# Retention and gated feed-forward on one core: eighteen sums of weight quarters dealt out anew on VectorE, and one ScalarE copy placed behind two one-column copies

## The chip, the core and the metric

The kernel runs on one core of a Trainium2 chip. A core has TensorE for matrix products (PE in the profile; its weight loads are listed apart as PEld), VectorE (DVE), ScalarE (ACT), GpSimd (POOL) and SyncE (SP, which here only issues transfers). Each engine takes its instructions in the order in which the program gives them and holds an instruction until what it needs is there. The metric is the device time of one launch in microseconds (us); lower is better.

## The reference

Two layers. The first is a retention layer: for each of 8 batches and 8 heads, 576 tokens of 64 columns, scores of queries and keys, weighted with a decay that is nought above the diagonal, times the values. The second is a feed-forward layer over the 4608 tokens that come of it, with a sigmoid gate.

```
scores = scale * np.matmul(q, k.transpose(0, 1, 3, 2))
gamma = 1.0 - 2.0 ** (-5.0 - np.arange(H, dtype=np.float32))
Dmat = np.where(rel >= 0, gamma[:, None, None] ** rel[None, :, :], 0.0)
attn_out = np.matmul(scores * Dmat[None, :, :, :], v)
x = np.ascontiguousarray(attn_out.transpose(0, 2, 1, 3)).reshape(B * S, H * D)
gate = 1.0 / (1.0 + np.exp(-(x @ w_gate)))      # 4608 x 512 times 512 x 1536
out = (gate * (x @ w_val)) @ w_out              # 4608 x 1536 times 1536 x 512
```

## The kernel before

**Retention.** The decay is split into a factor for each query and one for each key, which are multiplied into q and k when they are cast to bf16 (`cast_pair`, `cast_qk`). What is left of it is a mask of zeros and ones. Work goes by chunks of 128 tokens: products of k and q (`row`), the mask on VectorE (`mask`, L654; for the first three pairs of chunks `pair_qk`, L462), the product with v inside the chunk (`intra`, L665), a product with the running state of the chunks before (`inter`, L681), and a sum into that state (`add_state`, L774 to L780). The first three pairs of chunks are worked off before the loop; the third pair is prepared in lines 1448 to 1503. Its k, q and v are cast (`kp`, `qp`, `vp`), its masked scores are the tiles `ptp`, and `third_intra` (L533) is the product that reads them. `pair_st` (L476) is the product of `vp` and `kp`.

**Feed-forward.** The first 512 tokens are done by `h_both` and `op_first`. Behind them come blocks: two of 256 tokens (from token 512 and 768; numbers w = 0 and 1 in the loop of L1526) with plain products, then blocks of 512 tokens in which each product of two by two quarters is made of seven quarter products instead of eight. These want sums of quarters of the operands. The sums of weights are made once:

- `w_sums(kind, i, u, engine)` (L343, recorded as L349) makes the i-th sum of gate weights (kind g, tile `wgt_sb`) or of value weights (kind w, tile `wvt`) for the u-th third of the hidden columns. Each is one VectorE operation over 128x512 bf16.
- `wo_sums(i, u, 3)` (L316, recorded as L322) does the same for a third of the output weights (tile `wt_sb`).
- For i = 0, 1, 3 the sum goes to a tile of its own. The one with i = 2 is made in place on the weights and comes later, at the places listed in `PLACES`; the change leaves these.

**The order of VectorE's work.** `w_sums("g", i, 0)` and `("g", i, 1)` are made while the first 512 tokens are done (`step_sums`). Lines 1461 to 1463 make the three `("w", i, 0)`, ahead of the first output products and so ahead of the third pair's masks in VectorE's queue. The other eighteen stand in the list `weight_sums` (L1516). A block of 256 tokens runs through 18 turns (i = 0 to 17): twelve of hidden products (`h_units`, products `h_g` and `h_v`, VectorE's product L896) and six of output products (`op_units`, L1229). In each odd turn of w = 0 and w = 1 one sum is taken from the list (L1546). In the same turns the loop hands out the retention's pieces: a slot (`slot`) with its products and masks, and in the turns behind it the copies of the slot's values out of two PSUM banks (`leave_own` L750 on ScalarE, `leave_other` L766 on VectorE) and the state sums. The next slot's `intra` writes the same two banks.

**A block of 512 tokens.** `ORDER` (L1088) is a list written out by hand: products, sums, casts and cues. The entry `o` takes the next half of one of the output's seven products (`quarters`, L1127), in the order 1, 2, 6, 5, 7, 3, 4, into two banks a and e. `keep("16", a)` and `keep("5", e)` are ScalarE copies of 128x512 (L1139) from a bank to SBUF, which VectorE adds later (L1144). The entry `A` is a cue: the loop then gives two retention chunks (`slot_of_two`): `intra` and a part of `inter`, then two copies of a single column each on ScalarE (`glance`, L709), then the next chunks' scores, then the rest of `inter`. That rest writes the banks which the glances read, so TensorE does it only behind them. The second cue of a block comes right behind the second half of product 5.

The lines at the centre:

```
for i in (0, 1, 3):                                        # L1462
    w_sums("w", i, 0, nc.vector)
weight_sums = [... for kind, u in (("w", 1), ("g", 2), ("w", 2)) for i in (0, 1, 3)]
weight_sums += [lambda u=u, i=i: wo_sums(i, u, 3) for u in range(3) for i in (0, 1, 3)]
if w < 2 and i % 2 == 1 and weight_sums:                   # L1546
    weight_sums.pop(0)()
yield from product(5, e, True)                             # L1177
keep("5", e)
yield tail
```

Of the kernel before, what the change touches and what calls it, by code (L numbers as in the profile page):

```python
# [16 lines left out]
def kernel(  # L17
# [19 lines left out]
    nc = tc.nc  # L37
# [1056 lines left out]
    def quarters(gvs, sums, t0, k):  # L1094
# [38 lines left out]
        tail = W * (k * NFC // 2 - (k * NFC // 4 if k > 1 else 0))  # L1133
# [3 lines left out]
        def keep(name, ps):  # L1137
            kept[name] = sum_tile([P, 2, W], FP32, f"s{name}_{t0}", of=KEPT)[:, 0:k]
            nc.scalar.copy(out=kept[name], in_=ps)  # L1139
# [28 lines left out]
        if not final:  # L1168
            yield from product(2, e, False)
            for b in range(k):  # L1170
                obs[b] = osb.tile([P, DM], FP32, tag="osb", name=f"ob_{t0 + b * P}")
                nc.scalar.copy(out=obs[b][:, 0:W], in_=e[:, b])
            yield tail
            yield from product(6, a, False)
            keep("16", a)
            yield tail
            yield from product(5, e, True)  # L1177
            keep("5", e)
            yield tail
            yield from product(7, a, False)  # L1180
            add_half(1, 1, a, "5")
            yield tail
            yield from product(3, e, False)
            add_half(0, 1, e, "16")
            for b in range(k):
                stored(obs[b], places(b))
            yield tail
            yield from product(4, a, False)
            for b in range(k):
                nc.scalar.copy(out=obs[k + b][:, 0:W], in_=a[:, b])  # L1190
                stored(obs[k + b], places(k + b))
            ffn_psum.order = ffn_psum.held[::-1] + [x for x in ffn_psum.order if x not in ffn_psum.held]
            ffn_psum.held = []
            yield tail
            return
# [263 lines left out]
    step(units, 2)  # L1459
    loads_to(1)  # L1460
    value_sums_begin()
    for i in (0, 1, 3):  # L1462
        w_sums("w", i, 0, nc.vector)

    def op_first(fcs, nbs, opps):
        for fc in fcs:
# [46 lines left out]
    store(opps[3], 3 * P, on_act)  # L1513
    casts_to(1)

    weight_sums = [lambda kind=kind, u=u, i=i: w_sums(kind, i, u, nc.vector) for kind, u in (("w", 1), ("g", 2), ("w", 2)) for i in (0, 1, 3)]  # L1516
    weight_sums += [lambda u=u, i=i: wo_sums(i, u, 3) for u in range(3) for i in (0, 1, 3)]

    SPARE = {}
    for at, kind, u in PLACES:  # L1520
        SPARE.setdefault(at, []).append((lambda u=u: wo_sums(2, u, 3)) if kind == "o" else (lambda kind=kind, u=u: w_sums(kind, 2, u, nc.vector)))
# [4 lines left out]
    for w, (t0, n) in enumerate(BLOCKS):  # L1526
# [16 lines left out]
            twos = []  # L1543

        for i, cols in enumerate(ffn_units(t0, n, nxt)):
            if w < 2 and i % 2 == 1 and weight_sums:  # L1546
                weight_sums.pop(0)()
            if w == 1 and i == n_h + TURN_AT:
                turn_step(7)
            for x in SPARE.get((w, i - n_h if w == 1 else i), ()):  # L1550
                x()
            gone += cols
            pieces += 1
            if stores and (nxt is None or w + 2 == len(BLOCKS) and pieces % 4 == 0):
                leave()
            if n > 256 and i % 2 and i < n_h:
                continue
            if pending:
                pending.pop(0)()
            elif slots < end and gone * (end - begin) >= (slots - begin) * (total - 5 * 2048):  # L1560
                next_slot(slots)
                valued = slots - 1
                slots += 1
            elif twos and (cue if n == 512 else i - n_h >= 1):
                cue.clear()
                next_two(*twos[0], n == 512)
                valued = twos[0][0][-1]
                slots = max([slots] + [s + 1 for s in twos.pop(0)[1]])
# [34 lines left out]
```

## Time and profile before

| What | Value |
|---|---|
| median of 3 runs | 311.48 us (309.74 to 311.97) |
| the profiled execution, its own time | 310.14 us |
| span of the profiled execution | 308.4 us |
| TensorE busy | 297.8 us (97%) |
| VectorE busy | 248.7 us (81%) |
| ScalarE busy | 199.7 us (65%) |
| GpSimd busy | 208.2 us (67%) |
| first 512 tokens' output, third pair | about 38 to 52 us |
| blocks of 256 tokens (w = 0, w = 1) | about 52 to 72 us and 72 to 91 us |
| blocks of 512 tokens | from 91 us to the end |

Times inside the profile count from the span's start. A line of the timeline gives start, length, engine, line of the kernel, operation, what is written and read, the shape, the count of merged instructions, and in brackets the idle time of the engine before it with what ended it. A line of the waits gives the total, the number of times and the longest. Lengths of TensorE's pieces are modelled and overlap; the distance between two starts is the safer measure.

### The profile page before, as it was taken

The numbers are of one execution on the slowest core, as the hardware profiler recorded it, in microseconds if no ns is written. First come the engines' busy times: TensorE is split into PE (matmuls) and PEld (weight loads), VectorE is DVE, ScalarE is ACT, GpSimd is POOL, SyncE is SP. The second block draws the span as 40 slices with busy tenths as digits, with TensorE's granted clock in tenths as the row PEclk, the third lists the DMA queues.
The fourth block names the chain that finished last, engine by engine and source line by source line (L and its number), as shares of the span: only waits on it lengthen the run. The fifth ranks groups of instructions, "written<-read, shape, count | busy, mean of one in ns | idle before, by whom it ended". The sixth has DMA issues, their size and how long they took to land.

```text
span 308.4 us, 10693 instructions
## 1 busy us (share of the span) xinstructions
PE 297.8 (97%) x4361; PEld 243.0 (79%) x4370; DVE 248.7 (81%) x488; ACT 199.7 (65%) x454; POOL 208.2 (67%) x254
## 2 busy tenths in 40 slices
PE   8999999999999998999999999999999999999994
PEld 7664456867858887887888788888888888888883
DVE  5947966896899899689888988898789968945893
ACT  6755464536548665965796579757965796658640
POOL 5765655654566699669966996699769916751490
PEclk9999999999999999999999999999999999999999
DMA  7999999997999996994299729972871392012004
GB/s 212 315 364 374 359 287 241 221 189 169 216 213 233 257 203 120 284 238 109 55 253 223 157 47 275 199 170 38 207 184 23 38 294 84 2 53 88 1 3 136
DMA packets 144994, 55.00 MB, mean 178 GB/s; under 512 B 124336, under 2 KB 136880, under 8 KB 144944
## 3 DMA queue, kind: packets, MB, share of 16 engines
q1 hardware_dynamic: 144144, 53.66, 70.9%
q8 instruction: 34, 0.56, 0.7%
q10 hardware_dynamic: 800, 0.66, 0.7%
q14 instruction: 16, 0.13, 0.1%
HBM read 37.75 MB, written 9.44 MB: 153 GB/s over the span
## 4 chain that ended last, share of the span: by engine, by line
PE 81%; DVE 8%; SPq 4%; DMA 2%; issue 2%; POOL 1%; ACT 1%; DVEq 0%; ACTq 0%; POOLq 0%
PE wa L1015 11%; PE gatea L1015 11%; PE qa L1127 11%; PE qe L1127 8%; PE we L1015 6%; PE gatee L1015 5%; PE op L1468 3%; PE h_v L891 3%; PE h_g L891 3%; PE hv L1319 3%; PE wg L1015 3%; SPq L188 3%; PE gateg L1015 3%; PE hg L1319 2%; PE op L1229 2%; DMA wg<-in_moe_w_gate_dram 2%
## 5 line engine op out<-in xcount | busy, mean ns | idle before, releaser
L409 POOL TENSOR_TENSOR qk<-k,ktab 128x512 bf16<-128x512 f32 x30 | 32.4, 1080 | 22.0 <-DMA k<-in_k_dram 19.8
L1015 PEld LDWEIGHTS <-wg_sb 128*128 128x128 bf16 x336 | 32.7, 98 | 4.9 <-PE op L1229 0.8
L1127 PEld LDWEIGHTS <-gsum 128*128 128x128 bf16 x336 | 31.9, 98 | 5.6 <-issue 0.7
L1015 PEld LDWEIGHTS <-wv_sb 128*128 128x128 bf16 x336 | 32.8, 98 | 4.2 <-issue 0.3
L952 POOL TENSOR_TENSOR gsum<-gv 128x256 bf16<-128x256 bf16 (+1 forms) x34 | 25.9, 770 | 12.6 <-DVE gv L1038 11.4
L409 POOL TENSOR_TENSOR qk<-q,qtab 128x512 bf16<-128x512 f32 x28 | 31.2, 1115 | 1.7 <-DMA q<-in_q_dram 1.6
L1015 PEld LDWEIGHTS <-wgt_sb 128*128 128x128 bf16 x252 | 24.6, 98 | 4.0 <-issue 1.2
L654 DVE TENSOR_TENSOR pt<-row,tri 128x256 bf16<-128x256 f32 x60 | 21.4, 412 | 7.5 <-PE row L647 7.5
L1015 PEld LDWEIGHTS <-wvt 128*128 128x128 bf16 x252 | 24.6, 98 | 2.9
L952 POOL TENSOR_TENSOR gsum<-gv,gsum 128x256 bf16<-128x256 bf16 x39 | 26.9, 719 | 0.0
L1038 POOL TENSOR_TENSOR gv<-gv,wu 128x512 bf16<-128x512 bf16 x7 | 8.1, 1162 | 27.4 <-DVE wu L1064 27.4
L1127 PEld LDWEIGHTS <-gv 128*128 128x128 bf16 x240 | 22.9, 98 | 3.7 <-issue 0.8
L1015 PE MATMUL wa<-xsum,wv_sb 128*128 128x256 bf16 x168 | 25.2, 273 | 0.1
L1015 PE MATMUL gatea<-xsum,wg_sb 128*128 128x256 bf16 x168 | 24.1, 273 | 0.0
L615 ACT CAST sb<-s 128x256 bf16<-128x256 f32 x46 | 18.2, 414 | 5.7 <-DVE s L778 3.1
L729 ACT CAST xT<-val 128x256 bf16<-128x256 f32 x50 | 15.7, 387 | 6.4 <-PE val L681 6.4
L946 POOL TENSOR_TENSOR gsum<-gv 128x256 bf16<-128x256 bf16 (+1 forms) x16 | 14.4, 908 | 7.8 <-DVE gv L1038 7.8
L1038 POOL TENSOR_TENSOR gv<-gv,ws 128x512 bf16<-128x512 bf16 x14 | 16.3, 1164 | 2.6 <-DVE ws L1067 2.6
L1059 DVE TENSOR_TENSOR gatee<-gatea,gs 128x512 f32<-128x512 f32 x14 | 9.8, 697 | 9.6 <-PE gatea L1015 6.3
L1067 DVE TENSOR_TENSOR ws<-wa,ws 128x512 f32<-128x512 f32 x21 | 14.4, 685 | 3.9 <-PE wa L1015 3.9
L1067 DVE TENSOR_TENSOR gs<-gatea,gs 128x512 f32<-128x512 f32 x21 | 13.8, 687 | 4.4 <-PE gatea L1015 3.6
L1036 ACT ACTIVATE gv<-gs 128x512 bf16<-128x512 f32 x21 | 13.0, 629 | 6.5 <-DVE gs L1067 6.5
(182 smaller groups left out, 851.8 us busy)
## 6 DMA issues: line engine op xcount, KB each, us to landing
k<-in_k_dram SPq DMA_DIRECT2D x26, 256.0 KB, 4.0
q<-in_q_dram SPq DMA_DIRECT2D x26, 256.0 KB, 3.9
v<-in_v_dram SPq DMA_DIRECT2D x26, 256.0 KB, 4.2
out_dram<-ob SPq DMA_DIRECT2D x25, 256.0 KB, 3.1
wg<-in_moe_w_gate_dram SPq DMA_DIRECT2D x12, 256.0 KB, 5.2
wv<-in_moe_w_val_dram SPq DMA_DIRECT2D x12, 256.0 KB, 5.2
wo<-in_moe_w_out_dram SPq DMA_DIRECT2D x12, 256.0 KB, 5.0
v32p<-in_v_dram SPq DMA_DIRECT2D x6, 256.0 KB, 4.8
```

Source lines behind the costliest of these rows:

```text
L409: eng.tensor_tensor(out=natural_qk[s][:, i].rearrange("p m (y d) -> p y m d", y=2), in0=by_halves(loaded[s][1 - i]), in1=tab, op=ALU.mult)
L615: eng(out=state[key], in_=src)
L654: nc.vector.tensor_tensor(out=probs[s][:, y], in0=row_ps[s][y][:, 0], in1=tri.unsqueeze(1).to_broadcast([P, M, 64]), op=ALU.mult)
L729: nc.scalar.copy(out=x_out(ALL, cols_of(s, i)), in_=x_in(val_ps[s][i], cols_of(s, i)))
L891: nc.tensor.matmul(ps[:, i], lhsT=w_sb[:, kc, (fc + i) * P:(fc + i + 1) * P], rhs=xT(kc, slice(t0, t0 + n)), start=(kc == 0), stop=(kc == ...
L946: eng.tensor_tensor(out=s3, in0=a11, in1=a21, op=ALU.subtract)
L952: eng.tensor_tensor(out=to, in0=a, in1=b, op=op)
L1015: nc.tensor.matmul(ps[:, f], lhsT=w[:, kc, f * P:(f + 1) * P], rhs=x[:, kc], start=(first and f == 0 and kc == 0), stop=(f == 1 and kc == ...
L1038: eng.tensor_tensor(out=to, in0=to, in1=src, op=ALU.mult)
L1067: nc.vector.tensor_tensor(out=me["s5"], in0=a, in1=me["s5"], op=ALU.add)
L1127: nc.tensor.matmul(ps[:, b], lhsT=left(fp)[:, b * P:(b + 1) * P], rhs=right(fp), start=(first and fp == 0 and b == 0), stop=(fp == NFC // ...
L1319: nc.tensor.matmul(ps, lhsT=(wg_sb if what == "g" else wv_sb)[:, kc, fc * P:(fc + 1) * P], rhs=xT(kc, slice(0, 4 * P)), start=(kc == 0), s ...
```

## The change

1. The three `("w", i, 1)` are made together with `("w", i, 0)`, ahead of the first output products, and leave the list.
2. The list then holds fifteen sums: `("g", 2)`, `("w", 2)`, and nine of the output weights. They are taken at named turns instead of at each odd one: in w = 0 at 1, 3, 5, 9, 11, 13, 15, 16, 17, in w = 1 at 1, 3, 5, 7, 9, 11. So turn 7 of w = 0 loses its sum, turn 16 has one in addition, and the turns 13, 15 and 17 of w = 1 have none. At w = 0, turns 1, 3, 5 now make `("g", 2)` where `("w", 1)` was, and 9, 11, 13 make `("w", 2)`; the turns 15, 16, 17 make the first third of the output weights' sums.
3. In all blocks of 512 tokens but the last, `keep("5", e)` stands behind the yield that follows product 5. What the loop gives at that yield, the two glances among it, comes ahead of it in ScalarE's queue.

```diff
@@ quarters
             yield from product(5, e, True)
+            yield tail
             keep("5", e)
-            yield tail
             yield from product(7, a, False)
@@ before the first output products
     value_sums_begin()
-    for i in (0, 1, 3):
-        w_sums("w", i, 0, nc.vector)
+    for u in range(2):
+        for i in (0, 1, 3):
+            w_sums("w", i, u, nc.vector)
@@ ahead of the loop over the blocks
-    weight_sums = [lambda kind=kind, u=u, i=i: w_sums(kind, i, u, nc.vector) for kind, u in (("w", 1), ("g", 2), ("w", 2)) for i in (0, 1, 3)]
+    weight_sums = [lambda kind=kind, u=u, i=i: w_sums(kind, i, u, nc.vector) for kind, u in (("g", 2), ("w", 2)) for i in (0, 1, 3)]
     weight_sums += [lambda u=u, i=i: wo_sums(i, u, 3) for u in range(3) for i in (0, 1, 3)]
 
+    SUMS_AT = {0: (1, 3, 5, 9, 11, 13, 15, 16, 17), 1: (1, 3, 5, 7, 9, 11)}
@@ in the loop
         for i, cols in enumerate(ffn_units(t0, n, nxt)):
-            if w < 2 and i % 2 == 1 and weight_sums:
+            if i in SUMS_AT.get(w, ()) and weight_sums:
                 weight_sums.pop(0)()
```

## The prediction

> **What bounds the kernel now.** I read the page's first part first, then what TensorE waits for, then the timeline at each of those waits and at each place that the change touches.
>
> ```profile
> span 308.4 us, 10693 instructions
> ...
> PE 297.8 (97%) x4361; PEld 243.0 (79%) x4370; DVE 248.7 (81%) x488; ACT 199.7 (65%) x454; POOL 208.2 (67%) x254
> ```
>
> TensorE works without a break almost everywhere: 97% of the span. None of TensorE's work is removed, added or reordered here. So the change can give only what TensorE now loses in waiting at the touched places, and can cost only what new waiting it makes. The waits of TensorE, in the view of who waited for whom:
>
> ```profile
> PE val L681 <- ACT glance L709: 0.8, 1, 0.8
> PE qa L1127 <- DVE gsum L952: 0.8, 2, 0.6
> ...
> PE val L665 <- ACT xT L750: 0.4, 1, 0.4
> ...
> PE gatea L1015 <- DVE s L778: 0.4, 1, 0.4
> ...
> PE gatee L1015 <- DVE gatee L1059: 0.2, 1, 0.2
> ```
>
> All but the second (feed-forward sums, in the blocks of 512) lie in the stretch from 58 to 119 us, each at or behind something that is moved. These four add up to 1.8 us, 0.6% of the span: this is the size of the question. The losses behind a wait are a little larger than its idle time, as the first place shows.
>
> **Place one: the sum that leaves turn 7 of the first block of 256.** Timeline, an undisturbed slot first, then the disturbed one:
>
> ```profile
> 57.32 1.04 PE L891 MATMUL h_v<-xT,wv_sb 128*128 128x256 bf16 x8
> ...
> 58.29 0.32 PE L665 MATMUL val<-pt,v 64*64 64x64 bf16 x16
> ...
> 58.43 0.30 PE L681 MATMUL val<-T,sb 64*64 64x64 bf16 x16
> ...
> 61.57 1.04 PE L891 MATMUL h_v<-xT,wv_sb 128*128 128x256 bf16 x8
> 61.63 0.86 DVE L349 TENSOR_TENSOR wgt_sb<-wg_sb 128x512 bf16<-128x512 bf16 x1
> 61.77 0.60 ACT L894 ACTIVATE gv<-h_g 128x512 bf16<-128x512 f32 x1 [0.21 <-PE h_g L891]
> ...
> 62.73 0.27 ACT L750 CAST xT<-val 128x128 bf16<-128x128 f32 x1 [0.36 <-DVE xT L766]
> ...
> 63.04 0.54 PE L665 MATMUL val<-pt,v 64*64 64x64 bf16 x16 [0.44 <-ACT xT L750]
> ...
> 63.40 0.32 PE L681 MATMUL val<-T,sb 64*64 64x64 bf16 x16
> ```
>
> From the start of `h_v` to the start of `inter` it takes 1.11 us undisturbed (57.32 to 58.43) and 1.83 here (61.57 to 63.40): 0.72 lost. The rows name the cause: the sum of 0.86 us stands ahead of VectorE's copy out of the value banks, ScalarE's copy waits for that one, and the next chunk's product wants the banks. Without the sum, VectorE's copy starts at 61.63. ScalarE's still stands behind the sigmoid that ends at 62.37, so it ends near 62.6; the undisturbed `val` would start at 61.57 + 0.97 = 62.54. That leaves 0.07: the place gives **0.65** (bounds 0.3 and 0.72; the lower one if VectorE's copy is met by another delay of half the size of the sum's).
>
> **Place two: the value-weight sums in the turns 9, 11, 13.** The same dependence comes again one slot later, where a sum stays in front of the copies:
>
> ```profile
> 66.56 0.42 DVE L349 TENSOR_TENSOR wgt_sb<-wg_sb,wgt_sb 128x512 bf16<-128x512 bf16 x1
> ...
> 67.53 0.54 PE L665 MATMUL val<-pt,v 64*64 64x64 bf16 x16
> ...
> 67.88 0.25 PE L681 MATMUL val<-T,sb 64*64 64x64 bf16 x8
> ```
>
> From `val` to `inter` it takes 0.35 here against 0.14 at 58.29: the second bank is already late. Turn 11 now gets the second sum of `wvt` in place of this third one of `wgt_sb`; its form's shortest and longest are in the view by source line:
>
> ```profile
> L349 DVE TENSOR_TENSOR wvt<-wvt,wv_sb x3: 547/712/733, 39.8 to 69.6; 128x512 bf16<-128x512 bf16 x3
> ```
>
> So it is 0.13 to 0.31 us longer, and this falls on the path: I take a **cost of 0.2** (bounds 0 and 0.31). The extra sum of turn 16 lies in the output products of this block, ahead of an idle time of VectorE:
>
> ```profile
> 73.69 0.76 DVE L654 TENSOR_TENSOR pt<-row,tri 128x256 bf16<-128x256 f32 x2 [2.29 <-PE row L647]
> ```
>
> It lasts 0.4 to 1.26 us (below) and 2.29 us hide it. Cost 0; were that cover gone, its whole length would come onto the mask.
>
> **Place three: the end of the second block of 256.**
>
> ```profile
> 68.57 3.40 PE L1229 MATMUL op<-wo_sb,gv 128*128 128x512 bf16 x15 [0.16 <-issue]
> ...
> 71.81 1.04 PE L891 MATMUL h_g<-xT,wg_sb 128*128 128x256 bf16 x8
> ...
> 87.30 3.40 PE L1229 MATMUL op<-wo_sb,gv 128*128 128x512 bf16 x15 [0.16 <-issue]
> ...
> 88.86 1.26 DVE L322 TENSOR_TENSOR wt_sb<-wo_sb,wt_sb 128x512 bf16<-128x512 bf16 x1
> ...
> 90.49 0.42 DVE L778 TENSOR_TENSOR s<-s,row 128x256 f32<-128x256 f32 x1
> ...
> 91.06 1.03 PE L1015 MATMUL gatea<-xT,wg_sb 128*128 128x256 bf16 x8 [0.36 <-DVE s L778]
> ...
> 92.30 1.26 DVE L322 TENSOR_TENSOR wt_sb<-wo_sb,wt_sb 128x512 bf16<-128x512 bf16 x1
> ...
> 95.74 0.60 PE L1015 MATMUL gatee<-xT,wgt_sb 128*128 128x256 bf16 x4 [0.15 <-DVE gatee L1059]
> ```
>
> Fifteen output products take 3.24 from start to next start (68.57 to 71.81), so `gatea` was due at 87.30 + 3.24 = 90.54 and came at 91.06: 0.52 lost, to a state sum that ends at 90.91. The sum at 88.86 goes; the state sum then ends at 90.91 - 1.26 = 89.65 and is 0.9 early. At 95.74 `gatee` waits 0.15 more for an addition of VectorE, which by then is 2.5 us ahead, since the sum at 92.30 goes too. What is late next are the ScalarE copies that the same addition wants, and no row has TensorE waiting for them here. The place gives 0.52 + 0.15 = **0.67** (bounds 0.36, the idle time of the first wait alone, and 0.67).
>
> **Place four: the copy behind the looks.**
>
> ```profile
> 117.47 0.59 ACT L1139 COPY s<-qe 128x512 f32<-128x512 f32 x1
> ...
> 117.94 0.23 ACT L709 COPY glance<-val 128x1 f32<-128x1 f32 x2
> ...
> 118.23 0.32 PE L681 MATMUL val<-T,sb 64*64 64x64 bf16 x16 [0.78 <-ACT glance L709]
> ...
> 118.62 1.20 ACT L729 CAST xT<-val 128x256 bf16<-128x256 f32 x4 [0.45 <-PE val L681]
> ```
>
> The copy of bank `qe` stands in ScalarE's queue ahead of the glances. It is the one that moves, and the next ScalarE operation starts 0.47 later than it (117.47 to 117.94). So the glances start 0.47 earlier and TensorE goes on **0.47** earlier; the remainder of its 0.78 stays with what ScalarE has ahead of both. The added wait: the moved copy now stands behind glances that wait for TensorE's `inter`, and behind the copy stand ScalarE's four copies out of the value banks (118.62). They have 0.45 of idle ahead of them, which takes in nearly all of the 0.47. The moved copy's own readers, VectorE's additions and product 3 into bank e, come behind product 7. In the waits view this is the only glance that TensorE waits for, so the five other blocks give 0 (bounds 0 and 0.3 together, one or two of them at a wait of 0.2, the least that the rows above show).
>
> **Place five: three more sums ahead of the third pair's masks.**
>
> ```profile
> 39.31 0.42 DVE L349 TENSOR_TENSOR wvt<-wv_sb 128x512 bf16<-128x512 bf16 x1
> 39.37 0.83 POOL L312 CAST wo_sb<-wo 128x512 bf16<-128x512 f32 x1 [0.62 <-DMA wo<-in_moe_w_out_dram]
> ...
> 40.51 0.43 DVE L349 TENSOR_TENSOR wvt<-wv_sb,wvt 128x512 bf16<-128x512 bf16 x1
> ...
> 41.48 1.26 POOL L393 CAST vp<-v32p 128x512 bf16<-128x512 f32 x2
> ...
> 43.04 2.48 DVE L462 TENSOR_TENSOR ptp<-qkp,trip 128x512 bf16<-128x512 f32 x4 [2.11 <-PE qkp L455]
> ...
> 43.05 0.42 PE L476 MATMUL st<-vp,kp 64*64 64x64 bf16 x16
> ...
> 46.74 0.64 PE L533 MATMUL pvp<-ptp,vp 64*64 64x128 bf16 x32
> ```
>
> The three present ones take 39.31 to 40.94, 1.63 us. VectorE is idle for 2.11 us ahead of the masks, so three more end near 42.6 and the masks are not touched. At the longest form in the trace, 1.26 each, they would end at 44.7, the masks at 47.2, and `pvp` would be 0.5 late. The nearer cover is that of GpSimd: its two casts of `vp` end at 42.74, and `st` wants them at 43.05, 0.31 later. Beside the present sums a cast of the same shape takes 0.83, alone 0.63 (half of 1.26), so two of them may end 0.4 later, 0.1 past `st`. I take a **cost of 0.2**, since the cast that runs before them is lengthened too (bounds 0 and 0.5, the lock below apart; a gain is out, as nothing is taken away here).
>
> The Trainium skill, SBUF — State Buffer, section Who interferes with whom, says that a VectorE operation with both inputs in SBUF contends with a GpSimd operation that reads SBUF, and that the one that comes second is blocked outright. The 0.83 against 0.63 agrees in direction; by the rule the cost of this place would be nearer to the lock below than to 0.2.
>
> **The sum.** -0.65 + 0.2 - 0.67 - 0.47 + 0.2 = **-1.39 us**; with all bounds at their good ends -2.16 (0.72, 0.67, 0.47, 0.3 and no costs), with all at their bad ends -0.3 (0.3, 0.36 and 0.47, less 0.31 and 0.5). The profiled execution took 310.14 us, 1.74 more than its span; less 1.39 that is 308.75. It was 1.34 below the median of the runs shown, from which the same sum gives 310.1. I predict **309.4**, the middle of the two; the middle of the two times of before is 310.8.
>
> **The rivals.**
>
> *The gain is taken in again* (change 0, 310.8 by the same middle). TensorE comes earlier to the blocks of 512, and something there that does not move with it, a load or a GpSimd cast, makes it wait. For it: such a wait is there already, the 0.8 of `qa` for `gsum`. Against: it is the only one of that kind among the waits quoted, so at most it hides a part; and among those of TensorE from 40 us on no load is named.
>
> *The lock.* Sums and casts at place five run strictly one after the other. The three forms at their shortest are 0.42, 0.55 and 0.43, 1.4 together; `vp` then ends at 44.1 and `st` is 1.1 late in place of 0.2: 309.4 + 0.9 = 310.3. For it: the lengthened cast. Against: the cast that ran from 39.37 into the present sums was 0.2 longer, not longer by a whole sum.
>
> *The copy behind the looks becomes the bound* (slower). If in a block the moved copy delays ScalarE's copies by its full 0.59, and these delay TensorE through the value banks or the next block's first products, it costs 0.59 in each of six blocks, 3.5 in all: 309.4 + 3.5 = 312.9, or 2.1 us slower than before. It outweighs the gains of 1.39 from the third such block on. For it: the chain of dependence exists. Against: the 0.45 of idle ahead of those copies, which leaves 0.14 of the 0.59, 0.84 in six blocks.
>
> *More than the sum.* Every feed-forward sum that TensorE waits for (0.8 in the waits view) comes in time as well, and the five other looks give their 0.3: 1.1 more, 308.3. For it: VectorE comes freer out of the small blocks. Against: those two waits lie in blocks where the change moves nothing.
>
> **How the numbers follow.** Forecast 0.56, gain taken in 0.16, lock 0.10, copy 0.10, more 0.08. Within 1% (3.1 us) is about what a measurement of this kernel cannot tell from no change, and the runs shown already spread by 2.2. Faster by over 1% needs 3.1 us: the last rival's 2.5 and the forecast reach it only with the spread of the runs: 0.14. Slower by over 1% is the copy rival with more than 0.59 per block or an unforeseen wait: 0.09. Within 1%: 0.77. The range runs from 307.4, about the last rival from the lower profiled execution (310.14 - 2.5 = 307.6), to 311.7, which takes in the two rivals near no change with the runs' spread and leaves out the copy.
>
> **What would show it.** Right: at the slot near 62 us `val` follows `h_v` in about 0.97; at the end of the second small block `gatea` follows the outputs without a wait; the glances of the first block of 512 stand ahead of the `qe` copy and TensorE's wait there is near 0.3. The second `wvt` sum lies ahead of the late bank near 67 us, 0.2 worse. Wrong: a wait of `st` for `vp` of over 0.5, `pvp` waiting for masks, ScalarE's `xT` copies gating a product, or a stretch beyond 130 us that has become longer.

## The result, and the profile after

The changed kernel takes 309.01 us (median; 306.98 to 312.77), the kernel before, run beside it, 311.05 (309.17 to 312.32). The ratio is 0.9924 [0.9897, 0.9952]: 2.0 us less by the medians, 2.4 by the ratio, which leaves out two slow executions of the changed kernel (312.00 and 312.77). The forecast was 309.4 and 1.39 less. The profiled execution of the changed kernel took 309.74 us, span 308.0; that of before 310.14, span 308.4. So this pair of profiles differs by 0.4 us only, and one term in it has the opposite sign to the forecast.

The page's first part of the changed kernel, and then what its TensorE waited for (total, times, longest):

```profile
span 308.0 us, 10701 instructions
...
PE 297.9 (97%) x4370; PEld 243.1 (79%) x4370; DVE 251.9 (82%) x488; ACT 199.1 (65%) x454; POOL 206.7 (67%) x254
```

```profile
PE val L665 <- ACT xT L750: 1.2, 2, 1.0
...
PE qa L1127 <- DVE s L780: 0.9, 1, 0.9
PE qe L1127 <- issue: 0.9, 1, 0.9
...
PE val L681 <- ACT glance L709: 0.2, 1, 0.2
```

Of the four waits that the forecast rested on, both of the gate products are gone and the one behind the looks is down from 0.8 to 0.2. But `val` waits 1.0 at the place where the wait should have gone, and two waits near 144 and 176 us are longer. The pair of profiles stage by stage, each number the distance between two starts on TensorE, worked out from the timelines:

| From, to | before | after | difference |
|---|---|---|---|
| first output product to the first block of 256 (place five) | 13.67 | 13.66 | -0.01 |
| first block of 256 (places one, two) | 19.78 | 20.56 | +0.78 |
| second block of 256 up to `gatea` (place three) | 19.25 | 18.77 | -0.48 |
| `gatea` (91.06 before, 90.69 after) to the later `gatea` that reads `xsum` (96.61, 95.93; place three, second wait) | 5.55 | 5.24 | -0.31 |
| from there to the next block of 512 (place four) | 25.81 | 25.36 | -0.45 |
| from there to the last product | 180.45 | 181.14 | +0.69 |
| start of the span to the first output product | 38.36 | 37.70 | -0.66 |

The last row lies ahead of everything that is touched: it ran from 37.1 to 41.4 us in the profiles of this study (the two above 40 are told below). The five rows of the touched places come to -0.47 in this pair, and the stretch behind them gives 0.69 back: the pair of profiles doesn't show where the 2.0 us of the medians came from. The following fences are the timeline of the changed kernel at the five places.

Place one, turn 7 without its sum:

```profile
59.27 1.04 POOL L409 TENSOR_TENSOR qk<-k,ktab 128x512 bf16<-128x512 f32 x1 [1.03 <-DMA k<-in_k_dram]
...
59.41 1.95 DVE L811 COPY sf<-sbd 64x128 bf16<-64x128 bf16 x2
...
60.27 1.04 POOL L409 TENSOR_TENSOR qk<-q,qtab 128x512 bf16<-128x512 f32 x1
...
60.91 1.04 PE L891 MATMUL h_v<-xT,wv_sb 128*128 128x256 bf16 x8
...
62.31 0.28 DVE L766 TENSOR_TENSOR xT<-val,share 128x128 bf16<-128x128 f32 x1
...
62.94 0.55 PE L665 MATMUL val<-pt,v 64*64 64x64 bf16 x16 [1.00 <-ACT xT L750]
...
63.30 0.32 PE L681 MATMUL val<-T,sb 64*64 64x64 bf16 x16
```

From `h_v` to `inter` it takes 2.39, where it took 1.83 before and 1.11 is undisturbed. The sum is gone, but two small copies of the state ahead of that spot took 1.95 us in place of 0.38, and ScalarE's copy out of the value banks, which stands behind VectorE's, holds `val` for 1.00. So one sign that the prediction had named for being right (`val` 0.97 behind `h_v`) is 2.03 here, and one that it had named for being wrong, an `xT` copy of ScalarE that gates a product, is there, though not behind the copy that moved.

Place two and place three:

```profile
65.58 1.89 PE L1229 MATMUL op<-wo_sb,gv 128*128 128x512 bf16 x8
...
66.46 0.62 DVE L349 TENSOR_TENSOR wvt<-wvt,wv_sb 128x512 bf16<-128x512 bf16 x1
...
67.64 0.55 PE L665 MATMUL val<-pt,v 64*64 64x64 bf16 x16 [0.16 <-ACT xT L750]
```

```profile
87.22 3.63 PE L1229 MATMUL op<-wo_sb,gv 128*128 128x512 bf16 x16
...
90.69 1.04 PE L1015 MATMUL gatea<-xT,wg_sb 128*128 128x256 bf16 x8
...
95.05 0.60 PE L1015 MATMUL gatee<-xT,wgt_sb 128*128 128x256 bf16 x4
```

At two the `wvt` sum lasts 0.62 where the sum before it in that turn took 0.42, and TensorE waits 0.16 for it: the cost of 0.2 that was forecast. At three `gatea` and `gatee` follow without a wait.

Place four and place five:

```profile
116.78 0.22 ACT L709 COPY glance<-val 128x1 f32<-128x1 f32 x2
116.88 0.61 ACT L1139 COPY s<-qe 128x512 f32<-128x512 f32 x1
117.06 0.32 PE L681 MATMUL val<-T,sb 64*64 64x64 bf16 x16 [0.21 <-ACT glance L709]
```

```profile
39.52 1.36 POOL L393 CAST vp<-v32p 128x512 bf16<-128x512 f32 x2 [0.16 <-PE kTp L436]
39.67 0.74 DVE L349 TENSOR_TENSOR wvt<-wvt,wv_sb 128x512 bf16<-128x512 bf16 x1
...
42.38 0.43 DVE L349 TENSOR_TENSOR wvt<-wv_sb,wvt 128x512 bf16<-128x512 bf16 x1
42.39 0.42 PE L476 MATMUL st<-vp,kp 64*64 64x64 bf16 x16
42.72 2.48 DVE L462 TENSOR_TENSOR ptp<-qkp,trip 128x512 bf16<-128x512 f32 x4
...
46.08 0.64 PE L533 MATMUL pvp<-ptp,vp 64*64 64x128 bf16 x32
```

The looks now stand ahead of the `qe` copy. The six sums end at 42.81, the masks follow at 42.72 to 45.20, 0.9 us ahead of `pvp`; `vp` is ready at 40.88, 1.5 us ahead of `st`. Nothing is paid there. The looks are the `glance` rows.

### The profile page after: what moved, and what is told of

The parts are those of the page before. It is cut to its first block, busy times and chain, and to the rows that moved or that the text cites. A ratio compares the mean times of both kernels' runs of the same rounds, so it can differ in the third digit from the quotient of the medians.

```text
span 308.0 us, 10701 instructions
## 1 busy us (share of the span) xinstructions
PE 297.9 (97%) x4370; PEld 243.1 (79%) x4370; DVE 251.9 (82%) x488; ACT 199.1 (65%) x454; POOL 206.7 (67%) x254
## 4 chain that ended last, share of the span: by engine, by line
PE 87%; DVE 5%; SPq 2%; DMA 2%; issue 1%; ACT 1%; POOL 0%; DVEq 0%
PE gatea L1015 12%; PE wa L1015 12%; PE qa L1127 11%; PE qe L1127 8%; PE we L1015 6%; PE gatee L1015 6%; PE op L1469 3%; PE gateg L1015 3%; PE h_g L891 3%; PE op L1229 3%; PE wg L1015 3%; PE hg L1319 3%; PE hv L1319 3%; PE h_v L891 3%; SPq L188 2%; PE val L665 2%
## 5 line engine op out<-in xcount | busy, mean ns | idle before, releaser
L409 POOL TENSOR_TENSOR qk<-k,ktab 128x512 bf16<-128x512 f32 x30 | 32.3, 1078 | 19.2 <-DMA k<-in_k_dram 14.9
L409 POOL TENSOR_TENSOR qk<-q,qtab 128x512 bf16<-128x512 f32 x28 | 31.4, 1120 | 1.1 <-DMA q<-in_q_dram 1.1
```

Source lines behind the costliest of these rows:

```text
L409: eng.tensor_tensor(out=natural_qk[s][:, i].rearrange("p m (y d) -> p y m d", y=2), in0=by_halves(loaded[s][1 - i]), in1=tab, op=ALU.mult)
```

## The experiments

Each is compared with the kernel before on the same chip. The first four share one chip, the next four (from the changed kernel's repetition on) a second, the last four a third. On which chip the first comparison ran isn't known here; its kernel before took 311.05 us, those beside the experiments 311.37, 312.58 and 310.59. Profiles are of one execution each. The theory: the places give what they were priced at, about 1.4 us in all. The rivals: one part alone makes the gain; or the gain is taken in again by something that doesn't move with TensorE.

### One part alone

`copy_alone` is before with only the copy moved; `sums_alone` is the changed kernel with the copy put back.

```diff
--- copy_alone, against before
             yield from product(5, e, True)
-            keep("5", e)
             yield tail
+            keep("5", e)
--- sums_alone, against after
             yield from product(5, e, True)
-            yield tail
             keep("5", e)
+            yield tail
```

> Only the move of the copy of product 5 behind the looks; VectorE's sums as before. If the places of the prediction add up, about -0.5 us against before (ratio 0.998): TensorE's wait for the look near 118 us falls from 0.78 to 0.2-0.3, and the waits near 63 us (0.4), 91 us (0.4) and 96 us (0.2) stay. If the copy behind the looks costs something in the later blocks, the distance between the first products of two blocks beyond 122 us grows by up to 0.6 each and the time does not fall.

> All of the change but the copy. If the places add up, -0.9 to -1.6 us against before (ratio 0.995 to 0.997): no wait at the end of the second small block (0.4 and 0.2 before), the look's wait near 118 us stays at about 0.8. At 62 us the two theories differ: by the theory of the sums the wait for the value banks is below 0.1; by the theory of the port it is below 0.1 only where the two small state copies of VectorE (L811) last 0.2 each, and 0.7 to 1.1 where they meet a GpSimd cast and last about 1 us each.

Measured: `copy_alone` 311.82 us, ratio 1.0006 [0.9971, 1.0042]; `sums_alone` 312.53, 1.0039 [1.0007, 1.0072] (before on this chip: 311.37). Neither gains. In the profiles most of the part's own waits behave as forecast: with the copy alone the wait behind the looks falls to 0.3 and the 0.4 of `gatea` stays; with the sums alone both waits of the gate products and the one of `val` are gone and the looks' 0.8 stays. Two things came otherwise: with the copy alone `val` doesn't wait either (its sum lasted 0.42, see below), and the second wait of place three is gone although its sum stands where it stood (5.24 from `gatea` to the later `gatea`, as in the changed kernel). The 0.2 that is there lies at another product, at 97.33, behind the cast of v. Both profiles have something new instead: TensorE's `row` waits 0.4 for a DMA transpose (`T`), and ScalarE waits 0.7 and 0.4 for a load of v. `sums_alone` also began late, its first output product at 40.47, after a wait of 1.3 for a weight's cast. So the gain of single waits doesn't add up to time here. In the profiles a load takes its place; whether it does so in the median execution isn't shown (the profile of `copy_alone` is of its fastest, 309.65).

### The sum put back in turn 7

```diff
--- turn7_kept, against after
-    SUMS_AT = {0: (1, 3, 5, 9, 11, 13, 15, 16, 17), 1: (1, 3, 5, 7, 9, 11)}
+    SUMS_AT = {0: (1, 3, 5, 7, 9, 11, 13, 15, 17), 1: (1, 3, 5, 7, 9, 11)}
```

> The changed kernel, but the nine sums of the first small block in its odd turns, so that turn 7 has a sum and turn 16 none. By the theory of the sums, +0.5 to +0.7 us against the changed kernel, with a wait of 0.4 to 0.5 for the value banks near 62 us even where the small state copies are short. By the theory of the port the state copies decide: the wait is 0.4 with short copies and 1.4 or more with long ones.

Measured: 311.10 us, 0.9984 [0.9951, 1.0017]. The changed kernel was not run on this chip, so the 0.5 to 0.7 of time is not tested by this. The `val` wait is back, at 0.7, with the small copies at their short length, so the sum in turn 7 makes it. But how long it is differs from profile to profile. Here is the sum of this turn with GpSimd's cast of k beside it (the cast multiplies k by its factors, L409), in the timelines of `turn7_kept`, of `copy_alone`, and of before, where the prediction shows the sum (61.63, 0.86) but not the cast:

```profile
60.95 1.04 POOL L409 TENSOR_TENSOR qk<-k,ktab 128x512 bf16<-128x512 f32 x1 [1.76 <-DMA k<-in_k_dram]
61.07 1.04 PE L891 MATMUL h_v<-xT,wv_sb 128*128 128x256 bf16 x8
61.07 1.20 DVE L349 TENSOR_TENSOR wvt<-wv_sb 128x512 bf16<-128x512 bf16 x1
...
63.18 0.32 PE L681 MATMUL val<-T,sb 64*64 64x64 bf16 x16
```

```profile
61.41 1.04 PE L891 MATMUL h_v<-xT,wv_sb 128*128 128x256 bf16 x8
61.47 0.42 DVE L349 TENSOR_TENSOR wgt_sb<-wg_sb 128x512 bf16<-128x512 bf16 x1
61.84 1.04 POOL L409 TENSOR_TENSOR qk<-k,ktab 128x512 bf16<-128x512 f32 x1 [1.82 <-DMA k<-in_k_dram]
...
62.79 0.32 PE L681 MATMUL val<-T,sb 64*64 64x64 bf16 x16
```

```profile
61.17 1.04 POOL L409 TENSOR_TENSOR qk<-k,ktab 128x512 bf16<-128x512 f32 x1 [1.73 <-DMA k<-in_k_dram]
```

With `before_turns_apart`, which is told below:

| Kernel | sum starts | cast already running ends | sum ends | sum lasts | lost, `h_v` to `inter` less 1.11 |
|---|---|---|---|---|---|
| copy_alone | 61.47 | none yet | 61.89 | 0.42 | 0.27 |
| before | 61.63 | 62.21 | 62.49 | 0.86 | 0.72 |
| turn7_kept | 61.07 | 61.99 | 62.27 | 1.20 | 1.00 |
| before_turns_apart | 60.36 | 61.36 | 61.65 | 1.29 | 1.08 |

A sum that starts while a GpSimd cast runs ends 0.28 or 0.29 behind that cast; one that starts ahead of it lasts 0.42 and is left alone. What TensorE loses is the sum's length less 0.14 to 0.21. So the 0.72 that the forecast read was one draw out of 0.27 to 1.08, and the start of the cast, which waits for a load of k, sets which. Ten profiles of this study have no sum in that turn: eight of them lose 0.02 to 0.14 there, against the 0.07 of the forecast, and the two in which the small copies are held (the changed kernel's and `turns_and_v10`) lose 1.28 and 1.26.

### The small copies taken off VectorE

```diff
--- state_on_act, against after (L811)
-                (nc.vector.tensor_copy if hh == y else nc.sync.dma_start)(
+                (nc.scalar.copy if hh == y else nc.sync.dma_start)(
```

> The changed kernel with the two small copies of the first batch's state (64x128 bf16, SBUF to SBUF) on ScalarE in place of VectorE. By the theory of the port the wait for the value banks near 62 us is 0 to 0.2 whatever GpSimd does beside it, and the time falls by 0.3 to 1.0 us against the changed kernel (ratio to before 0.989 to 0.992). If the copies are not the cause of the 1.00 in the changed kernel's profile, that wait stays between 0.5 and 1 us and the time stays at 0.992.

Measured: 312.34 us, 1.0043 [1.0010, 1.0077]. The first block of 256 takes 19.10 in its profile, 1.46 less than in that of the changed kernel, and the `val` wait is gone, as expected. And yet the kernel is no faster, where 0.989 to 0.992 was expected. The execution in the profile took 314.45 us, 2.1 above this kernel's median, so it shows more of the loss than most. Its timeline shows where the time went in that execution: TensorE's row that wants the transposed tile `T` of the next chunk, and, some 25 us later, ScalarE's queue.

```profile
73.52 0.32 PE L639 MATMUL row<-T 64*64 64x64 bf16 x16 [0.99 <-DMA T<-qk]
...
98.02 0.62 ACT L414 CAST v<-v 128x512 bf16<-128x512 f32 x1 [2.45 <-DMA v<-in_v_dram]
98.54 0.58 ACT L997 COPY gs<-gatee 128x512 f32<-128x512 f32 x1
99.15 0.70 DVE L1059 TENSOR_TENSOR gatee<-gatea,gs 128x512 f32<-128x512 f32 x1 [2.52 <-ACT gs L997]
...
99.91 0.63 PE L1015 MATMUL gatea<-xsum,wg_sb 128*128 128x256 bf16 x4 [1.98 <-DVE gatee L1059]
```

The transpose was issued at 67.66 and landed 5.8 us later, at 73.47; `row` starts at 73.52. Then a cast of v stands in ScalarE's queue until its load is there, the copy `gs` stands behind it, VectorE's addition wants `gs`, and the gate product wants the bank: 2.45, 2.52, 1.98 are one wait seen from three engines. The chain ahead of `T` is load, GpSimd cast, transpose, `row`; how far TensorE sets its pace by freeing buffers isn't shown. In the profile of before the same `T` landed at 70.47 and was wanted at 73.05; in `copy_alone` it landed at 72.64 and was used at 72.68. The room in one execution is 2.6 us and in the next none.

### The changed kernel again, on the second chip

The same program, no edit.

> The changed kernel once more, on the chip of the three runs beside it. If the first ratio of 0.9924 is the change's own effect, it comes again within 0.989 to 0.996. If it held luck of the executions, it comes nearer to what the sum of the places gives, 0.9955, or to 1.

Measured: 312.30 us against 312.58 of before, 1.0003 [0.9973, 1.0033]. In its profile the small copies take 0.38 and there is no `val` wait; the first block of 256 takes 19.17. But:

```profile
94.91 0.62 ACT L414 CAST v<-v 128x512 bf16<-128x512 f32 x1 [0.84 <-DMA v<-in_v_dram]
...
95.43 0.58 ACT L997 COPY gs<-gatee 128x512 f32<-128x512 f32 x1
...
96.80 0.60 PE L1015 MATMUL gatea<-xsum,wg_sb 128*128 128x256 bf16 x4 [0.37 <-DVE gatee L1059]
...
100.82 0.60 PE L1015 MATMUL we<-xsum,wvt 128*128 128x256 bf16 x4 [1.24 <-DVE wu L1064]
```

Up to `gatea` 0.35 us of gain against the profile of before is there (52.35 from the first output product, against 52.70), with 0.3 lost at a `row` that waits for its `T`. From the later `gatea` to the next block of 512 it takes 27.41, against 25.81 before and 25.36 in the first profile of the changed kernel. The 0.37 is the wait for the load, passed on by `gs`. The 1.24 comes on top of it, and both together are more than the 0.84 that ScalarE waited. VectorE works without a break from 96.05 until `we` starts, and between the two waits it has these:

```profile
96.66 1.13 DVE L322 TENSOR_TENSOR wo_sb<-wo_sb 128x512 bf16<-128x512 bf16 x1
...
97.71 1.26 DVE L349 TENSOR_TENSOR wg_sb<-wg_sb 128x512 bf16<-128x512 bf16 x1
```

These are two of the sums made in place, which the change doesn't touch. In the profile of before they lasted 0.41 each (96.53 and 96.87) and were done when GpSimd's cast of k began at 97.17; here they start late, run beside the casts of k and q that began at 96.46 and 97.46, and take 1.57 longer together. In `six_more` the same two lasted 0.99 and 1.26 and `we` waits 1.1; in `sums_alone` the second lasted 1.26 and `we` waits 0.5. So in these rows the load's wait holds VectorE's addition (0.99 idle ahead of 96.05, for `gs`), and the larger part of the loss is that its sums then fall beside GpSimd's casts, as in turn 7.

The intervals of the two comparisons don't overlap: in the first the change is worth 0.8%, in the second nothing.

### Fewer sums

```diff
--- few_sums, against after
+    nc.vector.memset(wgt_sb[:, :, 2], 0.0)
+    nc.vector.memset(wt_sb, 0.0)
...
-    weight_sums = [... for kind, u in (("g", 2), ("w", 2)) for i in (0, 1, 3)]
-    weight_sums += [lambda u=u, i=i: wo_sums(i, u, 3) for u in range(3) for i in (0, 1, 3)]
+    weight_sums = [... for kind, u in (("w", 2),) for i in (0, 1, 3)]
...
+    SUMS_AT = {0: (15, 16, 17)}
```

> Leaves out twelve of the fifteen listed sums (the last third of the gate weights' and all of the output weights'; their tiles are filled with zeros at the start); the three of the value weights stand in the turns 15, 16, 17 of the first small block. VectorE has no sum in any other turn of the two small blocks. If VectorE's sums bound this stretch, from the first output product (L1469) to the first product of the blocks of 512 it takes 51.5 us or less, against 53.0 in the changed kernel's profile and 52.7 before. If the transposes and the loads ahead of them bound it, TensorE waits for a transpose (row L639 for DMA) and the stretch stays at 52.2 or more.

Measured: 317.74 us, 1.0154 [1.0109, 1.0199]. Of the two outcomes named, the second came (55.1 us for the stretch, `row` waiting), but it tells nothing of the sums. The zeroing stands at the start of VectorE's queue and holds the first cast of q, for which TensorE waits 2.2 us; the first output product comes at 41.41. `row` then waits 2.2 in all for `T`. A cost of my own edit.

### Transposes taken from the queue, in a turn's place

The k and q of chunks 4 and 5 are turned by TensorE instead of by DMA, in the steps that already do so for chunks 0, 1 and 7.

```diff
--- turns_on_pe, against after
-    TURNED = (0, 1, 7)
+    TURNED = (0, 1, 4, 5, 7)
...
+        if s + 1 in (4, 5):
+            pending.append(lambda: turn_step(s + 1))
```

> The changed kernel with the q and k of the chunks 4 and 5 turned by TensorE in place of the DMA transpose (two more turns, 0.45 to 0.55 us of TensorE each). If the transposes bind in most executions, no wait of a row product for DMA is left up to 85 us and the time falls against the changed kernel, by up to 0.5 us. If they do not, it rises by 0.9 to 1.1 us, the two turns.

Measured: 312.09 us, 0.9966 [0.9941, 0.9990], though TensorE has about 1 us more to do. No `row` wait, no wait of ScalarE for v. But the steps use the value banks, and TensorE waits 1.8 for VectorE's copy out of them, and 2.0 more at `val` with no releaser: a better place was wanted, and follows below. Against the changed kernel beside it this is 0.21 less by the medians, within the spread of either, where up to 0.5 less was expected.

### Three times as many sums at place five

```diff
--- six_more, against after
-    for u in range(2):
+    for u in (0, 1, 1, 1):
         for i in (0, 1, 3):
             w_sums("w", i, u, nc.vector)
```

The three second sums are made three times, with the same result each time.

> The changed kernel with the three sums ahead of the third pair's masks made three times (six more VectorE operations, the same result). By the rows the idle time ahead of the masks is used up by the first three; six more at 0.41 to 0.82 put the masks' end 2.5 to 4.9 us later. The product that reads them had 1.2 us of slack, so it waits 1.3 to 3.5 us, and the time rises by 1.0 to 3.5 us against the changed kernel. If GpSimd's casts of v are held up by VectorE's sums as by a lock, the products st wait too.

Measured: 312.96 us, 1.0003 [0.9972, 1.0034], by the medians 0.66 more than the changed kernel beside it. The stretch from the first output product to the first block of 256 is 15.44 instead of 13.66. The ratio is the same 1.0003 as the changed kernel's, so the 1.0 to 3.5 that was expected didn't come as time. TensorE waits 1.1 there, in three pieces, for the masks, and for nothing else that the waits name. `st` starts 4.69 behind the first output product, as in the changed kernel (37.70 to 42.39), and lasts 0.59 instead of 0.42: the second cast of `vp` ends 0.13 behind its start. So with twelve sums it is the masks that come late, and GpSimd's casts of `vp` hardly do.

### The loads taken off: the change with and without

This is the test of the sum. In the changed kernel and in before alike, chunks 4 and 5 are turned by TensorE through a PSUM bank that is free at that point, so that the late transposes are off the path in both.

```diff
--- turns_apart, against after; before_turns_apart, the same against before
-    TURNED = (0, 1, 7)
+    TURNED = (0, 1, 4, 5, 7)
+    def turn_apart(s):
+        t = att_pool.tile([P, 2, M, P], BF16, tag="T", name=f"T_{s}", bufs=6)
+        ps = st_psum.tile([P, 2, M, P], BF16, tag="st", name=f"apart_{s}")
+        for i in range(2):
+            for m in range(M):
+                nc.tensor.matmul(ps[:, i, m, :], lhsT=natural_qk[s][:, i, m, :], rhs=ident, is_transpose=True,
+                                 start=(i == 0 and m == 0), stop=(i == 1 and m == M - 1))
+        nc.scalar.copy(out=t, in_=ps)
+        turned[s] = t
...
+            if (w, i) in ((0, 17), (1, 5)):
+                turn_apart(4 + w)
```

> The changed kernel with the q and k of the chunks 4 and 5 turned by TensorE through the state's free PSUM bank (16 more transposes, about 0.9 us of TensorE) and copied by ScalarE, so two DMA transposes fewer. If the loads behind these transposes are the second bound that takes the gain in, no row product waits for DMA up to 85 us, ScalarE does not wait for the load of v near 95 us, and the ratio to before is 0.990 to 0.996 on a chip where the changed kernel alone gives 1.000. If they are not, it is 1.000 or more, the 0.9 us on top.

> The same two turns by TensorE in the kernel before. With the loads out of the way the waits of the kernel before for VectorE and for the look stand alone: against the run beside it that has the change, this one is slower by the sum of the places, 1.4 to 2.2 us (0.5 to 0.7%). If the change is worth nothing even then, the two are within 0.3 us.

Measured: 309.89 us (309.12 to 311.03) with the change and 311.52 (310.46 to 312.49) without; to the kernel before 0.9981 [0.9952, 1.0011] and 1.0025 [0.9999, 1.0050]. So the change is worth 1.63 us by the medians, 1.45 by the means of the twelve executions each (0.9 to 2.0 as an interval worked out from their spread), and 0.44% by the two ratios (0.44% of 310.59 is 1.4). That is what was expected of the pair. The other expectation, 0.990 to 0.996 of before, missed: the turns by TensorE cost time themselves, as `before_turns_apart` shows, and both kernels of the pair have 1.9 of waits at `val` near 175 and 211 us without a releaser. The changed kernel alone was not run on this chip. In the two profiles neither TensorE nor ScalarE's casts of v wait for a load or a transpose, and from the first output product on they are 1.77 apart: 0.00 at place five, -0.90 in the first block of 256, -0.24 and -0.19 at place three, -0.43 at place four, -0.01 behind. The forecast had +0.2, -0.45 (places one and two together), -0.67, -0.47 and 0 there. So the total is nearer to the forecast than its terms: the first block of 256 gave twice its share, and place three less, as a `turn` of the changed kernel waits 0.3 for VectorE there. TensorE's waits of the kernel without the change, and then with it:

```profile
PE val L692 <- issue: 1.9, 2, 1.2
...
PE val L676 <- ACT xT L761: 0.8, 1, 0.8
PE val L692 <- ACT glance L720: 0.8, 1, 0.8
...
PE gatea L1026 <- DVE s L789: 0.5, 1, 0.5
```

```profile
PE val L692 <- issue: 1.9, 2, 1.3
...
PE turn L600 <- DVE xT L777: 0.3, 1, 0.3
PE val L692 <- ACT glance L720: 0.3, 1, 0.3
```

### The cast that holds ScalarE moved to GpSimd

```diff
--- v10_on_pool, against after (L851)
-            cast_v(x, on_act if str(x % 4) in V_ON_ACT else on_pool)
+            cast_v(x, on_act if str(x % 4) in V_ON_ACT and x != 10 else on_pool)
```

> The changed kernel with the cast of chunk 10's v, near 95 us, on GpSimd in place of ScalarE. In the profiles where the gain was lost ScalarE stood there for 0.8 to 2.4 us until that v had landed, with a copy behind it that VectorE and then TensorE waited for (0.4 to 2.0 us). By the theory of the loads this wait of TensorE (gatea for gatee, we for wu) is gone, and the time falls by 0.3 to 1.5 us against the changed kernel's 1.000 on such a chip. If that wait was not the cause, the ratio stays at 1.000.

Measured: 307.94 us (306.81 to 311.47), 0.9911 [0.9887, 0.9935], the fastest of all. It was not run beside the changed kernel on one chip, so the distance between these two (0.9911 to 0.9924 and 1.0003) is not a measured pair. Nor was the kernel before run with this cast moved, so how much of the 0.9% is the move's own isn't shown. Its profile has the order of the changed kernel with the small copies undisturbed:

```profile
59.57 0.38 DVE L811 COPY sf<-sbd 64x128 bf16<-64x128 bf16 x2
...
60.63 1.04 PE L891 MATMUL h_v<-xT,wv_sb 128*128 128x256 bf16 x8
...
61.88 0.32 PE L681 MATMUL val<-T,sb 64*64 64x64 bf16 x16
```

`h_v` to `inter` takes 1.25: 0.14 is lost, where the forecast left 0.07. Against the profile of before its stretches are 0.00, -0.50, -0.32, -0.31, -0.44 and -0.03, -1.60 in all; no wait for a load is in it. The `T` of the next chunk landed at 71.36 and was used at 71.54.

### Both together

`turns_apart` and `v10_on_pool` in one kernel.

> Both at once: two chunks turned by TensorE and chunk 10's v cast by GpSimd. If each takes away its own part of the loads' hold, this is the fastest, 0.988 to 0.994 of before. If the turns already bring the loads in time, it equals the run with the turns alone.

Measured: 310.95 us, 1.0001 [0.9972, 1.0030]: slower than either. In its profile the small copies are held again (2.02 for the two) and `val` waits 1.0, and `val` has 2.4 us of waits between 170 and 260 us without a releaser that the profile shows (1.9 in `turns_apart`). Its profile is 4.05 longer than that of `v10_on_pool` from the first output product on: 1.67 in the first block of 256, where the copies are held, 0.72 in the second, and 1.48 in the stretch beyond the first block of 512. Why the copies are held and why `val` waits there stays open.

## Why the prediction was right, and where it wasn't

**The total** was forecast as -1.39 to 309.4 and came as 309.01, -2.0 by the medians. The pair without late transposes gives -1.63, the profile without load waits -1.60 against that of before. So the sum is borne out within 0.3 us in the kernels where no load binds. That is in part luck: in the pair the first block of 256 gave -0.90 for -0.45, which makes up for place three with -0.43 for -0.67; in the profile of the changed kernel itself the places come to -0.47; and its repetition on the second chip gave nothing. The prediction took 1% for about the least that a measurement of this kernel can tell; the interval here is 0.28% to either side, so the 0.8% of the first comparison is clear of no change.

**Place one** (-0.65, bounds 0.3 and 0.72). The mechanism was right: without the sum and with short copies 1.25 in `v10_on_pool`, and put back, the sum makes the wait again. Eight of the ten profiles without a sum in this turn lose 0.02 to 0.14, about the 0.07 that was left. The size was read from one execution as if the 0.86 belonged to the sum. It belongs to the sum and GpSimd's cast together: 0.27 to 1.08 was lost with the sum in place. And the step "VectorE's copy starts at 61.63" assumed that nothing ahead of it would be held; in the profile of the changed kernel the state copies were, and the place lost 1.28. That they were held is once more the two engines' meeting (last section), in the changed kernel and in `turns_and_v10`, and hardly in the other profiles; no run shows that the change makes it more or less likely.

**Place two** (+0.2, bounds 0 and 0.31). In the profile of the changed kernel 2.06 from the output products to `val` against 1.85 before, just the forecast, but by luck. In `v10_on_pool` and six other profiles the same sum takes 0.42, as the one before it in that turn did, and in `v10_on_pool` the cost is 0: again a matter of GpSimd's cast beside it, not of the form. The 0.55 that the prediction took for the form's shortest was a lengthened one.

**Place three** (-0.67): -0.79 in the pair of profiles, -0.63 in `v10_on_pool`, -0.43 in the pair without late transposes. The first wait is right: it is gone wherever the sum at 88.86 is gone. The second was read by its idle time, 0.15; by the starts `gatee` came 0.3 late (0.75 from `we` at 94.99 to 95.74, and 0.43 in the profile after), so -0.79 lies outside the bounds of 0.36 and 0.67. And it is not the change's alone: in `copy_alone`, whose sums stand as before, it is gone as well. That the copies of ScalarE would be late next was named there, with "no row has TensorE waiting for them here"; this is the chain that begins the loss in `after_again` and `state_on_act`, behind a load of v.

**Place four** (-0.47): -0.45, -0.44 and -0.43 in these three, and the stretch is 25.36 or 25.37 in every profile with the move in which TensorE isn't held near 96 us behind a cast that waits for its load. Right to a few hundredths, and the rival in which the copy becomes the bound shows in none of the profiles.

**Place five** (+0.2): 0 in the profile of the changed kernel, in `v10_on_pool` and in the pair; 0.18 at most with six sums (13.85 in `sums_alone`, where the two casts of `vp` last 0.61 each, as undisturbed, but wait for loads of v). The step that failed is the margin: `vp` was taken to end 0.31 ahead of `st`, as in that one execution, where two casts of a weight stood ahead of it. It had 1.5 us here, 0.9 in `turns_apart` and 0.15 in `v10_on_pool`, and `st` waited in none of them. And the lock, which I held against by "not longer by a whole sum", was there: the sum from 39.67 ends at 40.41, 0.28 behind the cast of 0.61 that had begun at 39.52. Both gave way in turn: the second cast ran 0.80 and ended 0.47 behind that sum. Both had the room.

**The rival that I underrated** is the gain taken in again (0.16). "Among those of TensorE from 40 us on no load is named" is true of the profile of before, and is a poor reason: a load that lands 2.6 us ahead of its use isn't in a view of waits, and that room is 4.4 in the profile of the changed kernel, 2.6 in that of before, and under 0.1 in `copy_alone` and `after_again`. On the second chip the gain was taken in. That it was by the rival's way is not shown: the room is gone in `copy_alone` too, where the sums stand as before and TensorE is no more than 0.4 us earlier at that row than in the profile of before. So the loads differ between executions by more than the change moves TensorE, and the change need not be what makes them bind. The views that would have told were the landing of each transpose against the start of the `row` that reads it, and ScalarE's queue at 95 us, where a cast that waits for a load stands ahead of copies that TensorE needs.

**The stretch beyond 130 us**, whose lengthening I had named as a sign of error, is 0.69 longer in the profile of the changed kernel: 0.9 at `qe` with no releaser and 0.9 at `qa` behind a state copy, where 0.6 and 0.6 were before. In the profiles of this study this stretch lasts from 180.09 us (`copy_alone`) to 181.90 (`turns_and_v10`), and the pair without late transposes shows no share of the change in it (-0.01). Its cause stays open.

Also open is why the same kernel gives 0.9924 in the first comparison and 1.0003 in the second. The wait for a load in the second one's profile, with the lengthened sums behind it, is a cause that fits; it is one execution's profile, and the pair that has no such waits was run on a third chip. What would settle it is the kernel before and the changed one, each with and without the moved cast, on one chip.

## What to carry to other kernels

Before summing the waits that a change removes, set beside each load on the next 30 us when it lands and when it is first wanted: room that is no larger than the sum can be a second bound, though no wait names it, and the room of one execution isn't that of the next. On an engine that works in order, a cast that waits for a load belongs behind the copies that TensorE needs, or on another engine. And the length of a VectorE operation beside GpSimd isn't its own: find the row of its form with GpSimd idle, and take the two as the ends of the range.

## What the runs showed of the hardware

**VectorE and GpSimd shut each other out for whole instructions.** A sum of 128x512 bf16 lasts 0.42 us with GpSimd idle. Started while a GpSimd operation runs, it ended 0.27 to 0.29 behind that one, in the profiles of before, the changed kernel and the experiments alike, and lasted up to 1.29. (It is never shorter than alone, also where the GpSimd operation was nearly done.) Conversely a GpSimd cast of 0.61 that starts in the first half of a sum ends 0.47 or 0.48 behind it: the 0.83 that the prediction read as a mild lengthening (39.37 to 40.20, the sum having ended at 39.73) is such a one. The small copies, 0.19 each, ended 0.06 and 0.05 behind the two casts beside them (60.37 and 61.36 against 60.31 and 61.31). The Trainium skill, SBUF — State Buffer, section Who interferes with whom, says that a VectorE copy in a two-port mode contends with GpSimd, as does an operation with two inputs in SBUF, and that the later one is blocked for the whole of the other's instruction. These rows agree with it, save that some 0.14 us of the blocked operation (0.42 less 0.28, 0.61 less 0.47) passes ahead of the other's end.

**A DMA transpose of one chunk** took 2.7 to 6.5 us from issue to landing over all the profiles, 25 to 27 of them in each, with medians from 3.9 to 4.3, and held the issuing queue for 1.23 to 4.09 us. This spread is larger than all that the change moved.
